# Gated linear attention and an MLP on one core: the last output tile's first half is copied out of PSUM by ScalarE instead of VectorE

## The chip, the cores and the metric

The kernel runs on one core of one Trainium2 chip. The metric is the device time of one execution in microseconds (us), as the median of several runs. A profile of one further execution tells where the time goes; its span runs from the first to the last instruction of the program.

## What is computed

The reference takes `q`, `k`, `v` and `f_logit`, each of 4 batches x 8 heads x 768 steps x 48 channels, and two weight matrices of 384 x 2048 and 2048 x 384, all float32:

```
f = 1 / (1 + exp(-f_logit))
for t in range(768):
    state = f[t, :, None] * state + outer(k[t], v[t])     # 48 x 48 per head
    y[t] = q[t] @ state
x = y with the heads of a step side by side               # 3072 x 384
h = x @ w_in                                              # 3072 x 2048
g = max(h, 0) ** 2
out = g @ w_out                                           # 3072 x 384
```

## The kernel before, in words

**The blocks.** The 768 steps are cut into six blocks of 128 steps; with the four batches a block has 512 columns (`NT`). For each block the attention part leaves x as three tiles of 128 rows (`NJ` = 3), each as a high and a low float16 part. The MLP then runs over 16 groups of 128 hidden channels (`NF` = 16, index `f`).

**The MLP of a block** is `Moe.run` (L354). For each `f`, `up` (L273) makes the hidden tile `ph` in PSUM with nine matmuls on TensorE (L295), `square` (L299) has ScalarE scale, clip, square and round it to `gh`, and `rest` (L335) has VectorE take the rounding remainder `gl`. Some steps later (`lag`), `down` (L344) multiplies `gh` and `gl` with the second weights and adds into three output tiles `po[0]` to `po[2]` in PSUM (L350), one for each 128 output channels (index `e`), nine matmuls for each `f`, three for each `e`. Each `po` is 128 x 512 float32 and fills one PSUM bank.

**The last block** ends in another order (L361 to L371). The `down` matmuls of its last seven `f` are held back and then run output tile by output tile: 21 matmuls for `e` = 0, 21 for `e` = 1, 21 for `e` = 2. Behind the matmuls of each `e` comes a step of the list `ends` (L996), and then the copy of `po[e]`, scaled, from PSUM to the tile `ob_last` in SBUF. `tails(e)` (L436) says in which pieces: one piece for `e` = 0 and `e` = 1, marked 1; for `e` = 2 two halves of 256 columns, the first marked 0 and the second marked 1. Before the change VectorE makes all four copies (L368).

**The flag and the branch.** The fast arithmetic holds for inputs of ordinary size. `verdict` (L1027) gathers on VectorE whether they are, and writes a flag (L1066). The third step of `ends`, which stands between the matmuls of `e` = 2 and the copies of `e` = 2, has every engine load the flag into a register (`values_load`, L999). After `fast_path` comes a branch on that register, `tc.If` (L1184), which every engine takes by itself: where the flag is set, a long general path runs, which has instructions for all engines; in the runs here it is skipped. Behind the branch the pieces of `ob_last` go out to DRAM (L1193), the piece marked 0 on ScalarE's DMA queue and the pieces marked 1 on SP's. Between the last product and the branch TensorE also runs 11 spare matmuls (L1016) whose results nobody reads. The program ends with a round of waits and drains on all engines, which the profile puts at L1250.

**What sets the order.** Each engine works through its own instructions in order. In this part of the kernel the order is that of the source; the written-out orders `FIRST` and `SECOND` concern the beginning only. The Tile framework adds the waits between engines. So on ScalarE the order near the end is: the last `square`, the flag load, the branch, the transfer of L1193; on VectorE: the last `rest`, the verdict, the copies of `e` = 0 and 1, the flag load, the two half copies, the branch.

Of the kernel before, what the change touches and what calls it, by code (L numbers as in the profile page):

```python
# [20 lines left out]
ALU = mybir.AluOpType  # L21
# [28 lines left out]
O_SCALE = 1.0 / (G_SCALE * W_SCALE)  # L50
# [54 lines left out]
class Moe:  # L105
# [248 lines left out]
    def run(self, hooks, obs=None, before=None, lag=LAG, hold=0, ends=()):  # L354


        for n in range(len(self.fs) + lag):
            if before and not obs and n == len(self.fs) + lag - 1:
                return
            self.at = n  # L360
            if obs and n == len(self.fs):  # L361
                for e in range(NJ):
                    for f in self.fs[-lag - hold :]:
                        self.down(f, (e,))
                    if e < len(ends):
                        ends[e]()
                    for _, cs in tails(e):
                        self.nc.vector.tensor_scalar(  # L368
                            out=obs[e][:, cs], in0=self.po[e][:, cs], scalar1=O_SCALE, scalar2=None, op0=ALU.mult
                        )  # L370
                return  # L371
            if n < len(self.fs):
                for hook in hooks.get((n, 0), ()):
                    hook()
                f = self.fs[n]
                self.up(f)
                self.square(f)
                for hook in hooks.get((n, 0.5), ()):
                    hook()
                self.rest(f)  # L380
                for hook in hooks.get((n, 0.7), ()):
                    hook()
            if before and n == 0:
                before()
                self.sums_of()
            if lag <= n < len(self.fs) - hold + (not hold) * lag:
                self.down(self.fs[n - lag])
            for hook in hooks.get((n, 1), ()):
                hook()
# [46 lines left out]
def tails(e):  # L436

    if e < NJ - 1:
        return ((1, slice(0, NT)),)
    return ((0, slice(0, NT // 2)), (1, slice(NT // 2, NT)))  # L440
# [814 lines left out]
```

## Time and profile before

| what | value |
|---|---|
| median of 3 runs | 457.17 us (456.66 to 457.46) |
| the profiled execution, its own time | 457.91 us |
| its span, first to last instruction | 456.2 us |
| TensorE matmuls busy | 447.8 us, 98% of the span |
| TensorE weight loads busy (beside the matmuls) | 225.2 us, 49% |
| ScalarE busy | 292.2 us, 64% |
| VectorE busy | 252.7 us, 55% |
| GpSimd busy | 77.9 us, 17% |
| granted TensorE clock, mean share of full speed | 0.996 |

The time of the profiled execution is longer than its span by 1.7 us, what lies before the first and after the last instruction. PE is TensorE's matmuls and PEld its weight loads, DVE is VectorE, ACT ScalarE, POOL GpSimd, SP the engine that issues most transfers. A name with a q (ACTq, DVEq) stands for that engine's sequencer: loads of registers, branches, semaphore instructions and the issuing of transfers, none of which count as busy. Matmuls follow each other in a pipeline, so their busy time tells little of how fast they run.

### The profile page before, as it was taken

The page shows a single profiled execution, that of the slowest core. Times are in us where ns is not written, and L with a number is a line of the kernel's source. Part 1 is how long each engine was busy: PE and PEld are TensorE (multiplying, and loading weights), DVE is VectorE, ACT ScalarE, POOL GpSimd, SP SyncE. Part 2 cuts the span into 40 slices and gives each one's busy share as a digit, 9 for nine tenths or more (in the row PEclk, how much of TensorE's full clock was granted, in tenths as well). Part 3 has the DMA queues.
Part 4 walks back from the last instruction along what each step waited for, and adds up shares of the span by engine and source line. Part 5 has one row for each costly group of instructions (what it writes and reads, how often), then busy time and mean ns, then how long its engine had stood idle before and what let it go on. Part 6 is the DMA issues. An engine that isn't in the chain of part 4 may idle for free.

```text
span 456.2 us, 11171 instructions
## 1 busy us (share of the span) xinstructions
PE 447.8 (98%) x4558; PEld 225.2 (49%) x4561; DVE 252.7 (55%) x445; ACT 292.2 (64%) x697; POOL 77.9 (17%) x126
## 2 busy tenths in 40 slices
PE   7999899999999999999999999999999999999998
PEld 3655554444454554545554455554455544444443
DVE  7999952879575656836434845535663322323131
ACT  4579856975566674767666877665975553765440
POOL 4446380898000000000000000000000000000000
PEclk9899999999999999999999999999999999999999
DMA  8988319551655424461243443144422000100002
GB/s 271 283 314 281 85 20 332 181 196 24 164 110 147 86 64 120 124 149 30 47 115 97 131 83 102 25 122 112 122 64 42 1 2 17 71 0 1 0 0 79
DMA packets 65821, 48.09 MB, mean 105 GB/s; under 512 B 47968, under 2 KB 51296, under 8 KB 65760
## 3 DMA queue, kind: packets, MB, share of 16 engines
q1 hardware_dynamic: 65168, 46.42, 36.2%
q0 software_dynamic: 448, 0.73, 0.7%
q8 instruction: 38, 0.62, 0.6%
q14 instruction: 23, 0.19, 0.1%
q10 hardware_dynamic: 144, 0.13, 0.1%
HBM read 35.84 MB, written 7.86 MB: 96 GB/s over the span
## 4 chain that ended last, share of the span: by engine, by line
PE 85%; ACT 4%; POOL 4%; DVE 3%; issue 2%; DMA 1%; SPq 0%; POOLq 0%; DVEq 0%
PE po L350 37%; PE ph L295 35%; PE ds L682 2%; POOL w L181 2%; PE ds L663 2%; POOL w L176 1%; PE py L746 1%; DMA vn<-in_vN_dram 1%; PE ph L756 1%; PE ph L746 1%; DVE fkq L552 1%; PE ds L675 1%; PE first_py L728 1%; PE py L756 1%; ACT head L162 1%
## 5 line engine op out<-in xcount | busy, mean ns | idle before, releaser
L295 PE MATMUL ph<-x,w 128*128 128x512 f16 x855 | 198.6, 379 | 0.6 <-DVE gl L337 0.6
L350 PE MATMUL po<-gh,w 128*128 128x512 f16 x570 | 169.7, 379 | 0.3 <-issue 0.3
L337 DVE TENSOR_TENSOR gl<-ph,gh 128x512 f16<-128x512 f32 x94 | 64.8, 690 | 180.0 <-ACT gh L316 180.0
L295 PEld LDWEIGHTS <-w 128*128 128x128 f16 x873 | 84.9, 98 | 102.9 <-issue 1.1
L350 PEld LDWEIGHTS <-w 128*128 128x128 f16 x864 | 82.8, 98 | 98.3
L312 ACT ACTIVATE ph<-ph 128x512 f32<-128x512 f32 x95 | 55.5, 584 | 111.9 <-PE ph L295 111.8
L350 PE MATMUL po<-gl,w 128*128 128x512 f16 x288 | 109.4, 380 | 0.0
L316 ACT ACTIVATE gh<-ph 128x512 f16<-128x512 f32 x94 | 56.1, 597 | 2.9
L313 ACT ACTIVATE ph<-ph 128x512 f32<-128x512 f32 x95 | 55.3, 582 | 3.0
L556 POOL TENSOR_SCALAR fkq<-fkq 128x8 f32<-128x8 f32 x18 | 12.7, 704 | 217.5 <-DVE fkq L552 102.1
L181 POOL TENSOR_TENSOR w<-wa,w 128x384 f16<-128x384 f32 x29 | 30.1, 1040 | 2.0
L176 POOL CAST w<-wa 128x384 f16<-128x384 f32 x29 | 19.8, 685 | 26.6 <-DVE wa L165 22.6
L552 DVE TENSOR_TENSOR_SCAN fkq<-fz,dr 128x520 f32<-128x520 f32 x18 | 23.1, 1282 | 1.9 <-ACT fz L545 1.3
L569 DVE TENSOR_TENSOR_SCAN fkq<-fz,dz 128x520 f32<-128x520 f32 x18 | 22.9, 1274 | 0.6
L165 DVE SCALAR_TENSOR_TENSOR wa<-raw,head 128x384 int32<-128x384 int32 (+1 forms) x33 | 22.9, 727 | 0.2 <-POOL w L181 0.2
L599 ACT COPY sx<-sp 48x208 f32<-48x208 f32 x40 | 14.5, 363 | 12.5 <-DVE sp L712 11.8
L746 PE MATMUL py<-sc,vn 64*48 64x64 f32 (+1 forms) x384 | 21.0, 222 | 0.4 <-DVE sc L697 0.3
L746 PEld LDWEIGHTS py<-sc,vn 64*48 64x48 f32 (+1 forms) x384 | 16.4, 126 | 8.9 <-issue 7.7
L162 ACT ACTIVATE head<-raw 128x384 f16<-128x384 bf16 (+1 forms) x33 | 20.2, 636 | 0.6 <-DMA raw<-in_w_dram 0.5
L756 PE MATMUL py<-rx,sx 48*48 48x64 f32 x192 | 19.9, 216 | 0.2
L316 ACT ACTIVATION_READ_ACCUMULATOR gh<-ph 128x1 f32 x94 | 18.3, 194 | 0.0
L746 PE MATMUL ph<-sc,vn 64*48 64x64 f32 (+1 forms) x256 | 16.6, 222 | 0.0
(146 smaller groups left out, 479.1 us busy)
## 6 DMA issues: line engine op xcount, KB each, us to landing
raw<-in_w_dram SPq DMA_DIRECT2D x33, 383.8 KB, 6.0
fkq<-in_fkqT_dram SPq DMA_DIRECT2D x15, 768.0 KB, 5.3
vn<-in_vN_dram SPq DMA_DIRECT2D x24, 192.0 KB, 4.4
kn<-steps SPq DMA_DIRECT2D x14, 224.0 KB, 3.2
steps<-fkq SPq DMA_DIRECT2D x48, 64.0 KB, 2.2
out_dram<-ob SPq DMA_DIRECT2D x12, 256.0 KB, 2.3
fkq<-in_fkqT_dram SPq DMA_DIRECT2D x9, 256.0 KB, 5.6
last_kq<-fkq SPq DMA_DIRECT2D x28, 64.5 KB, 2.9
```

The costliest lines, as they stand in the source:

```text
L162: nc.scalar.mul(out=self.upper(head, F16), in_=high, mul=TOP_SCALE)
L176: eng.tensor_copy(out=w[:, 0], in_=a)
L181: (eng or nc.vector).tensor_tensor(out=w[:, 1], in0=a, in1=high, op=ALU.subtract)
L295: self.nc.tensor.matmul(self.ph[f], lhsT=w[:, i], rhs=x[:, j], start=first and n == 0, stop=last and n == 2)
L312: nc.scalar.activation(ph, ph, AF.Relu, scale=R_SCALE if self.half else 1.0)
L313: nc.scalar.activation(ph, ph, AF.Square)
L316: nc.scalar.activation(gh, ph, AF.Copy, accum_out=self.sums[:, n : n + 1])
L337: self.nc.vector.tensor_tensor(out=gl, in0=self.ph.pop(f), in1=gh if self.half else gh.bitcast(F32), op=ALU.subtract)
L350: self.nc.tensor.matmul(po[e], lhsT=l, rhs=r, start=f == fs[0] and i == 0, stop=f == fs[-1] and i == 2,)
L552: V.tensor_tensor_scan(out=rr[:, ::-1], data0=self.fz[:, NZ * CZ : 0 : -1], data1=dr[:, ::-1], initial=0.0, op0=ALU.mult, op1=ALU.add,)
L746: nc.tensor.matmul(self.py[c][h * C : h * C + m, b * C : (b + 1) * C], lhsT=self.vn[rows, b, h * D : h * D + m], rhs=self.sc[rows, h, b], ...
L756: nc.tensor.matmul(self.py[c][h * C : h * C + m, b * C : (b + 1) * C], lhsT=s[rows, b * D : b * D + m], rhs=q[rows], start=False, stop=b = ...
```

## The change

In the last block, the piece marked 0 is copied by ScalarE (`nc.scalar.mul`), the pieces marked 1 by VectorE as before. Only `e` = 2 has a piece marked 0, so of the four copies one changes its engine.

```diff
@@ -364,10 +364,14 @@
                         self.down(f, (e,))
                     if e < len(ends):
                         ends[e]()
-                    for _, cs in tails(e):
-                        self.nc.vector.tensor_scalar(
-                            out=obs[e][:, cs], in0=self.po[e][:, cs], scalar1=O_SCALE, scalar2=None, op0=ALU.mult
-                        )
+                    for late, cs in tails(e):
+                        ob, po = obs[e][:, cs], self.po[e][:, cs]
+                        if late:
+                            self.nc.vector.tensor_scalar(
+                                out=ob, in0=po, scalar1=O_SCALE, scalar2=None, op0=ALU.mult
+                            )
+                        else:
+                            self.nc.scalar.mul(out=ob, in_=po, mul=O_SCALE)
                 return
```

## Rows read from the trace of the kernel before

**Rows 1.** The profile page: its first line.

```profile
span 456.2 us, 11171 instructions
```

**Rows 2.** The chain that ended last, 440 to 457 us: start, us, what.

```profile
442.73 9.06 PE po L350 x42
...
451.84 2.35 PE spare L1016 x10
```

**Rows 3.** Timeline, 452.2 to 453 us: start, us, engine line op, [idle before <-releaser].

```profile
451.83 0.76 DVE L368 TENSOR_SCALAR ob_last<-po 128x256 f32<-128x256 f32 x2 [3.84 <-PE po L350]
...
452.28 0.37 ACTq L1193 DMA_DIRECT2D out_dram<-ob_last  x1
452.61 0.33 SPq L1193 DMA_DIRECT2D out_dram<-ob_last  x1
```

**Rows 4.** Groups of instructions by shape, whole span: count | busy us, mean ns.

```profile
L777 ACT CAST x<-py 112x256 f16<-112x256 f32 x12 | 4.6, 385 | 0.0
...
L409 ACT ACTIVATE ob<-po 128x512 f32<-128x512 f32 x8 | 4.3, 593 | 0.0
...
L472 ACT ACT_TABLE_LOAD x1 | 1.3, 1283 | 0.8 <-PEq L1241 0.8
...
L368 DVE TENSOR_SCALAR ob_last<-po 128x256 f32<-128x256 f32 x2 | 0.8, 420 | 3.8 <-PE po L350 3.8
```

**Rows 5.** DMA issues by line: count, KB each, median us from issue to landing.

```profile
out_dram<-ob_last ACTq DMA_DIRECT2D x1, 128.0 KB, 2.1
out_dram<-ob_last SPq DMA_DIRECT2D x1, 128.0 KB, 2.0
```

**Rows 6.** What SP's queue waited for: us in total, times, longest.

```profile
SPq L1250 <- DVEq L1184: 0.3, 1, 0.3
```

**Rows 7.** The branch, L1184, 451.5 to 455: ns min/median/max, first and last start.

```profile
L1184 PEldq COMPARE_BRANCH  x1: 3356/3356/3356, 450.1 to 450.1; - x1
L1184 DVEq COMPARE_BRANCH  x1: 72/72/72, 451.8 to 451.8; - x1
L1184 PEldq EVENT_SEMAPHORE  x1: 51/51/51, 454.2 to 454.2; - x1
L1184 DVEq EVENT_SEMAPHORE  x1: 21/21/21, 454.7 to 454.7; - x1
```

**Rows 8.** Timeline, 440 to 457 us.

```profile
439.84 0.19 ACT L316 ACTIVATION_READ_ACCUMULATOR gh<-ph 128x1 f32 x1
...
440.07 0.69 DVE L337 TENSOR_TENSOR gl<-ph,gh 128x512 f16<-128x512 f32 x1 [1.25 <-ACT gh L316]
...
447.30 0.69 DVE L368 TENSOR_SCALAR ob_last<-po 128x512 f32<-128x512 f32 x1 [3.30 <-PE po L350]
...
447.85 5.09 SPq L1193 DMA_DIRECT2D out_dram<-ob_last  x3
```

**Rows 9.** The flag load, L999: ns min/median/max, first and last start.

```profile
L999 ACTq TENSOR_LOAD <-flag x1: 467/467/467, 443.4 to 443.4; - x1
...
L999 DVEq TENSOR_LOAD <-flag x1: 542/542/542, 447.3 to 447.3; - x1
```

**Rows 10.** The branch, L1184, 443 to 447.65.

```profile
L1184 SPq EVENT_SEMAPHORE  x8: 17/17/17, 447.1 to 447.6; - x8
L1184 ACTq COMPARE_BRANCH  x1: 50/50/50, 444.0 to 444.0; - x1
L1184 POOLq COMPARE_BRANCH  x1: 50/50/50, 444.0 to 444.0; - x1
L1184 SPq COMPARE_BRANCH  x1: 50/50/50, 444.3 to 444.3; - x1
L1184 ACTq EVENT_SEMAPHORE  x1: 17/17/17, 446.4 to 446.4; - x1
```

**Rows 11.** The end of the program, L1250, 444 to 454.65.

```profile
L1250 POOLq DRAIN  x1: 1284/1284/1284, 444.5 to 444.5; - x1
L1250 ACTq DRAIN  x1: 148/148/148, 452.7 to 452.7; - x1
```

## The prediction

> **What bounds the kernel now.** I read the page first, for the span [rows 1], then the chain of waits at the end, then the timeline of each engine there, then the rows of the flag load (L999), of the branch (L1184), of the last transfers (L1193) and of the program's end (L1250). The reader is to see two things.
>
> First, TensorE works without a gap up to the last product: the chain holds 42 L350 matmuls in 9.06 us and leaves them at 451.8 [rows 2]. All the change can touch is what comes after, 456.2 - 451.8 = 4.4 us, and what it puts ahead of a queue that somebody waits for.
>
> Second, that tail is no plain sum of copy and transfer. VectorE's two half copies start at 451.83, each 0.42 us long and overlapping to 0.76 us in all [rows 3, 4]; the first half leaves on ScalarE's queue at 452.28 and the second on SP's at 452.61 [rows 3]. ScalarE's transfer lands 2.1 us after its issue, at 454.4, and SP's 2.0 after, at 454.6 [rows 5]. But SP also waits 0.3 us for VectorE's first semaphore behind the branch [rows 6], which comes at 454.7 although VectorE branched at 451.8 [rows 7]: 2.9 us in which VectorE has nothing recorded. What follows, to 456.2, is the closing round of waits of all engines. So today **VectorE's branch** sets the end, 0.1 to 0.3 us behind the transfers.
>
> **The change, step by step.**
>
> *The first half moves to ScalarE.* Removed: one VectorE copy. VectorE's remaining copy can start at 451.83 instead of behind the first, so it ends some 0.34 us earlier (0.76 less one copy of 0.42), and SP's transfer goes out at about 452.3. By the rows above this is worth nothing: VectorE's branch was already issued at 451.8, together with its first copy and not after its second [rows 3, 7], and that branch ends last. Even given back in full, 0.34 us is under what can be told from no change: 0.2% here is 0.91 us.
>
> *The copy itself.* ScalarE's nearest row is its cast of 112x256 elements out of PSUM, 0.39 us [rows 4]; I take that (0.59, its scaled copy of twice the size at L409, is the upper end). Its function tables were loaded once in the whole program [rows 4], while it has run the scaled copy of L409 eight times for `ob` among its other functions, so no second load is due: 0. ScalarE's last work today ends at 440.03 [rows 8], so no compute is displaced.
>
> *What it is put ahead of.* This is where the cost lies. ScalarE's order today is: load the flag (443.4, 0.47 us) [rows 9], branch (444.0), its first semaphore behind the branch (446.4) [rows 10], then stand at L1193 until VectorE has copied. All this runs beside TensorE's last 8 us and costs nothing. In the source the copy stands behind the flag load and ahead of the branch, so the branch now stands behind an instruction that waits for the last matmul. An engine here passes on to its next instruction only when the one that waits has started: VectorE's flag load is at 447.3, beside its second copy at 447.30, and its branch at 451.8, beside the copy at 451.83 [rows 3, 7 to 9]. So I put ScalarE's branch at 451.85 instead of 444.0.
>
> Behind it stands the time to the first instruction on the other side. The rows have it for ScalarE over the same skipped code: 446.4 - 444.0 = **2.4 us**. The others: SP 2.8 (444.3 to 447.1), POOL 0.5 (444.0 to a drain at 444.5), VectorE 2.9, TensorE 4.1 (450.1 to 454.2, of which part is its wait for the spare matmuls) [rows 7, 10, 11]. I take ScalarE's own. Bounds: 0.5 below, 4.1 above. Then two or three semaphore steps to the transfer: SP shows 447.6 to 447.85, so 0.2 [rows 8, 10].
>
> The sum: 451.85 + 2.4 + 0.2 = 454.45 for ScalarE's transfer, against 452.28; landing 2.1 later, 456.55. SP goes through its waits one by one, 0.07 us each where nothing is outstanding (eight in 447.1 to 447.6 [rows 10]); I count one such step from the landing's wait to where it is free of VectorE's. Today SP is through VectorE's wait at about 454.75, and 456.2 - 454.75 = 1.45 us are left. So the end is 456.55 + 0.07 + 1.45 = 458.1, **1.9 us later**. ScalarE's own closing drain, today at 452.7 [rows 11], comes at about 455 and holds nobody.
>
> The span goes from 456.2 to 458.1 and the profiled execution's own time from 457.91 to 459.8. That execution lies 0.74 us above the median of the three runs, 457.17; put on the median, 1.9 us give **459.1**.
>
> *Do the two copies run side by side?* No row shows two engines reading one PSUM bank together; both halves lie in one bank. Side by side costs nothing; one behind the other, in source order, VectorE would start at 451.83 + 0.39 + 0.04 (the handoff from ScalarE's 440.03 to VectorE's 440.07 [rows 8]) = 452.26. Its branch moves by 0.43 and its first semaphore to 455.1, still ahead of 456.55. So the sum stands either way; the other order would put ScalarE's branch 0.43 us later.
>
> The Trainium skill ("PSUM — Partial Sum Buffer", section "PSUM bank collisions raise a hardware error") speaks against the change here: two engines may not touch one bank of the same partitions together, reads included, and the accesses should be guarded "by bank × quadrant". By that rule VectorE's half has to wait for ScalarE's and the split brings no parallel copying. No row of this trace decides it; the sum is the same by both.
>
> **The rivals.**
>
> *1. The branch is short, and nothing is lost (not slower).* Place: between ScalarE's branch and its transfer. It decides whether ScalarE's landing passes VectorE's 454.7: if branch and semaphores together take under 0.5 us, the transfer is out by 452.6 and the end stays at 456.2. Up to 1.4 us the loss stays under 0.91. For it: POOL went on 0.5 us behind the same branch [rows 10, 11], and ScalarE now stands 8 us ahead of the branch in which something could be got ready. Against: ScalarE itself took 2.4 us, and VectorE took 2.9 after standing 3.84 us ahead of its branch [rows 3, 7]. POOL has next to nothing in the skipped code, ScalarE has loops of activations there. The time: 457.2; with copies one behind the other VectorE's branch ends the kernel 0.43 us later, 457.6.
>
> The Trainium skill ("Runtime: NRT & Kernel Launch", section "Instruction fetch mechanics") has fetching ahead as purely sequential, so that a taken branch to a target outside the window waits for a transfer. By that, standing ahead of the branch helps nothing and only the distance skipped counts, which speaks for 2.4 us and against this rival.
>
> *2. Three branches at once.* ScalarE's and VectorE's branches fall together at 451.8, with TensorE's, begun at 450.1, still open for 3.36 us [rows 7]. If they hold each other up, ScalarE's takes VectorE's 2.9 (+2.4 us, 459.6) or at most TensorE's 4.1 (+3.6 us, 460.8). For it: today SP, which branched 0.3 us after ScalarE, needed 2.8 against 2.4. Against: in that crowd ScalarE's own was the 2.4.
>
> *3. Another order.* Were the flag load also put behind the copy on ScalarE, another 0.47 us would follow: +2.4, 459.6. The load's place in the source and VectorE's order speak against it.
>
> *4. Faster.* By 0.91 us I find no mechanism; only a different order elsewhere in the program, from the moved instruction, could do it.
>
> **How the numbers follow.** The forecast, 459.1, has 0.70, with its own range of 458.6 to 459.6 (the rounding of the rows and the spread of 0.8 us among the runs before). Rivals 2 and 3 have 0.14 together, rival 1 with both prices 0.13, rival 4 0.03. So slower by over 0.2% is 0.84, within 0.2% 0.13, faster 0.03. 0.2%, 0.91 us, is about what a measurement of this kernel tells from no change. The range starts at 458.0, the edge of that, leaving out rivals 1 and 4, and ends at 460.8, the upper bound of the branch.
>
> **What would show it.** Right: ScalarE's copy at L368 at about 451.8, its branch beside it, its first semaphore behind the branch at 454.2 to 454.7, its transfer at about 454.5 instead of 452.28, SP's longest closing wait on that landing and no longer on VectorE, and a tail of 6.3 us behind the last matmul where 4.4 stood. SP's transfer should go out earlier, at 452.3 (or at 452.7 with the copies one behind the other). Wrong: ScalarE's branch still near 444.0, or its transfer before 453; or the span unchanged with VectorE's semaphore last as now. If the branch takes 2.4 and the end still doesn't move, my reading of who ends last is false.

## The result, and the profile after

The changed kernel takes 460.46 us (median of 4 runs, 460.33 to 460.76) against 457.08 us before (also the median of 4 runs, one more than in the table ahead of the prediction), a ratio of 1.0076 (95% interval 1.0064 to 1.0088): 3.4 us slower. The forecast was 459.1, 1.9 us slower. The direction held, and so did the whole range, 458.0 to 460.8; the size is nearly twice the forecast's and lies outside 458.6 to 459.6, the range that the forecast gave to its own sum. Line numbers behind the change are four higher than in the kernel before: L999 is L1003 now, the branch L1184 is L1188, the transfers L1193 are L1197, the closing waits L1250 are L1254.

The first line of the page, which answers to [rows 1]:

```profile
span 458.6 us, 11171 instructions
```

ScalarE's and VectorE's copies and the transfers of the last tile, from timelines of single engines and of the end of the span (start us, us, engine line op, [idle before <-releaser]). They answer to [rows 3]:

```profile
450.55 0.38 ACT L374 ACTIVATE ob_last<-po 128x256 f32<-128x256 f32 x1 [11.79 <-PE po L350]
...
450.56 2.35 PE L1020 MATMUL spare<-one 128*128 128x512 bf16 x10
450.96 0.42 DVE L370 TENSOR_SCALAR ob_last<-po 128x256 f32<-128x256 f32 x1 [4.26 <-ACT ob_last L374]
451.42 0.33 SPq L1197 DMA_DIRECT2D out_dram<-ob_last  x1
453.35 2.32 ACTq L1197 DMA_DIRECT2D out_dram<-ob_last  x1
```

Two things are to be seen. VectorE's half does not run beside ScalarE's: it starts 0.41 us later, and its releaser is ScalarE's copy. And ScalarE's transfer goes out 2.8 us behind the start of the first copy instead of 0.45, and takes **2.32 us to issue** where it took 0.37.

The rows of the branch (ns min/median/max, first and last start), which answer to [rows 7, 10]:

```profile
L1188 PEldq COMPARE_BRANCH  x1: 3416/3416/3416, 448.9 to 448.9; - x1
L1188 ACTq COMPARE_BRANCH  x1: 50/50/50, 450.6 to 450.6; - x1
L1188 DVEq COMPARE_BRANCH  x1: 72/72/72, 451.0 to 451.0; - x1
L1188 PEldq EVENT_SEMAPHORE  x1: 51/51/51, 453.0 to 453.0; - x1
L1188 ACTq EVENT_SEMAPHORE  x1: 17/17/17, 453.1 to 453.1; - x1
L1188 DVEq EVENT_SEMAPHORE  x1: 21/21/21, 453.8 to 453.8; - x1
```

ScalarE's branch now stands beside its copy, and 2.5 us pass to its next instruction. The landings (KB, us from the start of the issue) answer to [rows 5], SP's longest closing wait to [rows 6]:

```profile
out_dram<-ob_last SPq DMA_DIRECT2D x1, 128.0 KB, 2.1
out_dram<-ob_last ACTq DMA_DIRECT2D x1, 128.0 KB, 3.7
```

```profile
SPq L1254 <- DMA out_dram<-ob_last: 4.8, 1, 4.8
```

SP ends on that landing, at 453.35 + 3.7 = 457.05, and no longer on VectorE.

Executions differ by up to 2.2 us in what lies before the last product: over all traces of this document, the first read of the finished last tile starts between 450.42 and 452.66 us (at 451.83 in the profile before and at 450.55 in this one). So below I also compare the **tail**, the span less the start of the first instruction that reads the finished last tile: 456.2 - 451.83 = 4.4 us before and 458.6 - 450.55 = 8.1 us now. The tail is 3.7 us longer, the medians 3.4. One run of all those below, of the kernel with the transfer on another queue, took 938.18 us where its nine others took 456.95 to 458.11, and is left out of every ratio.

### The profile page after: what moved, and what is told of

It reads as the page before. It is cut to its first block, busy times and chain, and to the rows that moved or that the text cites. A ratio compares the mean times of both kernels' runs of the same rounds, so it can differ in the third digit from the quotient of the medians.

```text
span 458.6 us, 11171 instructions
## 1 busy us (share of the span) xinstructions
PE 447.2 (98%) x4558; PEld 224.8 (49%) x4561; DVE 252.1 (55%) x444; ACT 292.7 (64%) x698; POOL 77.9 (17%) x126
## 4 chain that ended last, share of the span: by engine, by line
PE 82%; DVE 6%; POOL 4%; DMA 2%; ACT 2%; issue 2%; SPq 0%; POOLq 0%; DVEq 0%; ACTq 0%
PE po L350 37%; PE ph L295 35%; PE ds L686 2%; POOL w L181 2%; PE ds L667 2%; DMA raw<-in_w_dram 2%; DVE fkq L556 2%; POOL w L176 1%; PE py L750 1%; DVE fkq L573 1%; PE ph L760 1%; PE ph L750 1%; DVE wa L165 1%; PE py L760 1%; ACT head L162 1%
```

## The experiments

Two questions were open. Is it the branch behind the copy that costs (theory 1), or the copies themselves (rival 2)? And why did the transfer take 2 us more to issue? The numbers of theories and rivals in this section are those of the experiments' own expectations; the prediction's rivals are other ones.

**The transfer on another queue.**

```diff
-            (nc.sync if n else nc.scalar).dma_start(out[NBLK - 1, e * P : (e + 1) * P, cs], obs[e][:, cs])
+            nc.sync.dma_start(out[NBLK - 1, e * P : (e + 1) * P, cs], obs[e][:, cs])
```

> The changed kernel, but the first half of the last tile leaves on SP's queue, which has branched long before. ScalarE still copies it and still branches late. Theory 1 (what costs is that ScalarE's transfer stands behind ScalarE's branch): nothing waits for ScalarE's branch any more, both transfers are out by 1 us behind the last product, and the end is set by VectorE's branch, which starts 0.4 us later than before because its copy waits for ScalarE's: 457.3 to 457.7. Rival 2 (what costs is the copy on ScalarE and VectorE's wait for it): the time stays near 460.4.

Measured: 457.82 us (457.78 without the run of 938.18) against 456.83 for the kernel before in the same session, ratio 1.0022 (1.0012 to 1.0032). Its last two transfers, its branches and what SP waited for:

```profile
451.12 0.90 SPq L1197 DMA_DIRECT2D out_dram<-ob_last  x2
```

```profile
L1188 ACTq COMPARE_BRANCH  x1: 50/50/50, 450.7 to 450.7; - x1
L1188 DVEq COMPARE_BRANCH  x1: 72/72/72, 451.1 to 451.1; - x1
...
L1188 DVEq EVENT_SEMAPHORE  x1: 21/21/21, 454.3 to 454.3; - x1
```

```profile
SPq L1254 <- DVEq L1188: 1.7, 1, 1.7
```

ScalarE copies and branches as late as in the changed kernel, and 2.4 of the 3.4 us are gone: theory 1 holds, rival 2 falls. What is left, 1.0 us, is a little more than expected (457.3 to 457.7). VectorE's branch sets the end here: it starts 0.4 us behind the first copy, and takes 3.2 us to its semaphore, 0.3 more than before.

**The wait alone.** The kernel before, with one added ScalarE instruction behind the flag load:

```diff
-            lambda: general.append(nc.values_load(general[0][0:1, 0:1], min_val=0, max_val=1)),
+            lambda: (general.append(nc.values_load(general[0][0:1, 0:1], min_val=0, max_val=1)), nc.scalar.mul(out=moe.const.tile([P, 1], F32, name="column"), in_=moe.po[2][:, :1], mul=O_SCALE)),
```

> The kernel before, VectorE making all copies, with one added ScalarE instruction ahead of the branch: it scales one column (128x1) of the last output tile out of PSUM into a place that nobody reads. So ScalarE waits for the last product, and no copy changes its engine. Theory 1: ScalarE's branch comes 7.9 us later as in the changed kernel, and the first half leaves as late as there: 460.1 to 460.7. Rival 2: VectorE's copies come about 0.25 us later behind the small one, nothing else: 457.3.

Measured: 460.67 us, ratio 1.0081 (1.0064 to 1.0098), no different from the changed kernel. The profiled execution is the longest of its four (462.54); what it has more lies before the last product, and its tail is 460.8 - 452.66 = 8.1 us as in the changed kernel. In its trace ScalarE's read of one column and its transfer, VectorE's copies, and ScalarE's branch and first semaphore:

```profile
452.66 0.17 ACT L999 ACTIVATE column<-po 128x1 f32<-128x1 f32 x1 [11.79 <-PE po L350]
455.49 2.39 ACTq L1193 DMA_DIRECT2D out_dram<-ob_last  x1
```

```profile
452.86 0.76 DVE L368 TENSOR_SCALAR ob_last<-po 128x256 f32<-128x256 f32 x2 [4.04 <-ACT column L999]
```

```profile
L1184 ACTq COMPARE_BRANCH  x1: 50/50/50, 452.7 to 452.7; - x1
...
L1184 ACTq EVENT_SEMAPHORE  x1: 17/17/17, 455.3 to 455.3; - x1
```

No copy has changed its engine here. An instruction of 0.17 us that waits for the last product ahead of ScalarE's branch is enough for the whole loss. VectorE's copies wait for it too, 0.2 us, although it writes a tile of its own: what the two share is `po`, which both only read.

**The copy behind the branch.** The reverse: ScalarE copies, but branches early.

```diff
-                            self.nc.scalar.mul(out=ob, in_=po, mul=O_SCALE)
+                            self.owing = ob, po
...
+        ob, po = moe.owing
+        nc.scalar.mul(out=po, in_=ob, mul=1 / O_SCALE)
+    ob, po = moe.owing
+    nc.scalar.mul(out=ob, in_=po, mul=O_SCALE)
```

The first two added lines at the end stand inside the skipped general path, the last two behind the branch; the PSUM pool of this tile is opened outside the fast path so that it lives on (lines left out here).

> The changed kernel with ScalarE's copy moved behind the branch (the PSUM tile is kept until then; the general path, which is skipped, puts its own result back into it). ScalarE branches early again, at about 443 to 444. Its copy now stands behind VectorE's in the source, so it would run 0.45 us behind the last product, and its transfer goes out at 0.9 us behind it. Theory 1 with theory 3 (first transfer slow where its engine has not stood at it): issue of 2.3 us and a landing 3.7 us after it, 458.3 to 458.9. Theory 1 with rival 4 (slow only right behind a branch): issue of 0.4 us, 456.9 to 457.4. Rival 2: near 460.

Measured: 456.99 us against 456.83, ratio 1.0001 (0.9991 to 1.0012). The timelines of VectorE and ScalarE:

```profile
450.81 0.42 DVE L370 TENSOR_SCALAR ob_last<-po 128x256 f32<-128x256 f32 x1 [3.84 <-PE po L350]
```

```profile
451.31 0.39 ACT L1196 ACTIVATE ob_last<-po 128x256 f32<-128x256 f32 x1 [12.30 <-DVE ob_last L370]
451.73 0.37 ACTq L1201 DMA_DIRECT2D out_dram<-ob_last  x1
```

The whole loss is gone with ScalarE still copying, and here too the copies run one behind the other, VectorE's first. The transfer, the only one that ScalarE issues in the program, takes 0.37 us although ScalarE had not stood at it: so a transfer is not slow for being the first on its queue.

**An earlier transfer on ScalarE's queue.** The changed kernel with:

```diff
-            lambda: None,
+            lambda: nc.scalar.dma_start(aside.tile([P, C], F32, name="unread"), mask),
```

> The changed kernel, with one small transfer (128 x 64 float32 from SBUF to a scratch place in DRAM that nobody reads) issued on ScalarE's queue ahead of the flag load, while ScalarE is idle. The slow issue at the end was 2.32 us where it had been 0.37. Theory 3 (the first transfer of the program on a queue is slow to issue, unless its engine has stood at it before): the last one is now the second, 0.4 us, lands 2.1 us after its issue, and the time falls by 1.6 to 2.0 us to 458.4 to 458.9. Rival 4 (it is slow because it comes right behind a branch): 460.4 as before.

Measured: 460.02 us, ratio 1.0078 (1.0061 to 1.0095). ScalarE's two transfers in its timeline:

```profile
437.95 0.34 ACTq L1002 DMA_DIRECT2D unread<-mask  x1
...
453.26 2.13 ACTq L1197 DMA_DIRECT2D out_dram<-ob_last  x1
```

The first transfer of the queue takes 0.34 us and the second, behind the branch, 2.13. Theory 3, that a queue's first transfer is slow, falls; what is left is rival 4, the branch just ahead.

**The branch by itself, without the crowd.** The kernel before; ScalarE reads a column of the middle tile ahead of its branch, and the first tile goes out on its queue.

```diff
-            lambda: general.append(nc.values_load(general[0][0:1, 0:1], min_val=0, max_val=1)),
+            lambda: (general.append(nc.values_load(general[0][0:1, 0:1], min_val=0, max_val=1)), nc.scalar.mul(out=moe.const.tile([P, 1], F32, name="column"), in_=moe.po[1][:, :1], mul=O_SCALE)),
...
-            (nc.sync if n else nc.scalar).dma_start(out[NBLK - 1, e * P : (e + 1) * P, cs], obs[e][:, cs])
+            (nc.sync if n and e else nc.scalar).dma_start(out[NBLK - 1, e * P : (e + 1) * P, cs], obs[e][:, cs])
```

> The kernel before, with an added ScalarE read of one column of the middle output tile ahead of ScalarE's branch, so that this branch comes about 4 us before the end of the products, with no other engine's branch open, and with the transfer of the first output tile put on ScalarE's queue, its data ready long before. What is read is how long that transfer, ScalarE's first behind the branch, takes to issue. Theory 5 (a transfer soon behind a branch is slow by itself): 2.0 to 2.5 us. Rival 6 (it is slow because ScalarE's, VectorE's and TensorE's branches fall together): 0.3 to 0.6 us. The time itself stays near 457 by both, since the transfer of the last tile's first half waits for its data anyway.

Measured: 458.82 us in one run (456.94 before). The rows of the branch and of ScalarE's two transfers (ns min/median/max, first and last start):

```profile
L1184 ACTq COMPARE_BRANCH  x1: 50/50/50, 447.1 to 447.1; - x1
L1184 PEldq COMPARE_BRANCH  x1: 3376/3376/3376, 449.2 to 449.2; - x1
L1184 ACTq EVENT_SEMAPHORE  x1: 17/17/17, 449.9 to 449.9; - x1
```

```profile
L1193 ACTq DMA_DIRECT2D out_dram<-ob_last x2: 405/1268/2132, 450.1 to 452.4; - x2
```

ScalarE branches 2.1 us before TensorE and 3.8 us before VectorE, and the first transfer behind its branch still takes 2.13 us, the next 0.41. TensorE's and VectorE's branches are open by the time of this transfer, but so they are in the run with the copy behind the branch (449.1 and 450.8), where it took 0.37. Rival 6, the crowd, falls. The time missed what both had given it, near 457: the last tile's first half, issued in 0.41 us, landed only 3.7 us later. Why is open.

**Both halves on ScalarE's queue.** The changed kernel with `(nc.sync if e < NJ - 1 else nc.scalar)` at L1197.

> The changed kernel with both halves of the last tile leaving on ScalarE's queue, one behind the other. Theory 5, in the form that the first transfer behind the branch pays once: first issue 2.0 to 2.4 us, second 0.3 to 0.5 us, time 460.5 to 461.2. If each transfer near the branch pays: two slow issues, 462.0 to 463.0. Rival 6 gives the same as the first form, since the branches still fall together.

Measured: 460.23 us in one run, a little under the expected band.

```profile
L1197 ACTq DMA_DIRECT2D out_dram<-ob_last x2: 384/1204/2023, 453.6 to 455.7; - x2
```

The first transfer behind the branch pays 2.02 us, the second 0.38.

**Small work between branch and transfer.** The changed kernel with eight, then 32 one-column copies:

```diff
+    for n in range(8):
+        nc.scalar.mul(out=sums[:, n : n + 1], in_=obs[0][:, n : n + 1], mul=1.0)
```

> The changed kernel with eight one-column ScalarE copies (of the first output tile, into a place that nobody reads afterwards) between ScalarE's branch and its transfer, some 1 to 1.5 us of work. Theory 5a (something for the transfer arrives a fixed time behind the branch): the copies run at once at some 0.17 us each, the transfer's issue is shorter by what they took, 0.8 to 1.3 us, and the time stays at 460.0 to 460.7. Theory 5b (the first transfer behind the branch costs 2 us whenever it comes): the issue stays at 2.1 to 2.4 us and the time is 1 to 1.5 us longer, 461.2 to 462. If the copies themselves stall for some 2 us, it is not the transfer but any instruction there.

> The run with eight small ScalarE copies behind the branch, with 32 of them, 0.09 us apart, some 2.9 us in all. There the issue of ScalarE's transfer began earlier or later in the runs but ended 4.8 to 5.2 us behind ScalarE's branch each time. Theory 5a (a transfer of ScalarE can't go out before about 5 us behind its branch, other work can): the copies run without a stall, the transfer begins at 5 to 5.7 us behind the branch and its issue takes 0.3 to 0.6 us. Rival 7 (the stretch of code itself arrives in two pieces, and what stands some way behind the target waits, whatever it is): one of the copies stands still for 1 to 2 us.

Measured: 460.5 us with eight (456.94 before) and 461.38 us with 32 (456.87 before), one run each. ScalarE's timeline of the one and of the other:

```profile
453.71 0.48 ACT L1195 ACTIVATE sums<-ob_last 128x1 f32<-128x1 f32 x4 [2.35 <-ACTq L1188]
454.07 1.83 ACTq L1199 DMA_DIRECT2D out_dram<-ob_last  x1
454.10 0.47 ACT L1195 ACTIVATE sums<-ob_last 128x1 f32<-128x1 f32 x4
```

```profile
451.80 0.38 ACT L374 ACTIVATE ob_last<-po 128x256 f32<-128x256 f32 x1 [11.79 <-PE po L350]
454.49 2.24 ACT L1195 ACTIVATE sums<-ob_last 128x1 f32<-128x1 f32 x23 [2.31 <-ACTq L1188]
456.55 0.37 ACTq L1199 DMA_DIRECT2D out_dram<-ob_last  x1
456.64 0.93 ACT L1195 ACTIVATE sums<-ob_last 128x1 f32<-128x1 f32 x9
```

The copies never stall. With eight of them the transfer begins 3.1 us behind the branch, not 2.8, and its issue is 1.83 us, 0.5 shorter; with 32 it begins 4.75 us behind ScalarE's branch (at 451.80, beside its copy) and takes 0.37. Theory 5a holds, that ScalarE's transfer does not get out before about 5 us behind the branch while other work runs; rival 7, that the code behind the branch arrives in two pieces and whatever stands in the second has to wait, falls. In the seven kernels where a ScalarE transfer comes soon behind ScalarE's branch, the issue ends at 5.1, 5.0, 5.2, 5.2, 4.8, 4.9 and 5.1 us behind the branch (the changed kernel, the early transfer, the wait alone, the branch by itself, both halves, eight copies, 32 copies).

**SP made to wait instead of ScalarE.** The kernel before, with a small SP transfer ahead of the branch, of 64 columns of the last tile's first half:

```diff
-                moe.run(hooks[k], obs, owed, LAST_LAG, HOLD, ends)
+                moe.run(hooks[k], obs, owed, LAST_LAG, HOLD, ends); nc.sync.dma_start(aside.tile([P, C], F32, name="unread"), obs[NJ - 1][:, :C])
```

> The kernel before, with one small transfer on SP's queue ahead of the branch that reads the first half of the last tile out of SBUF into a scratch place in DRAM that nobody reads. So SP, and not ScalarE, stands ahead of its branch until the last product is copied; three large transfers wait behind SP's branch, two of them with their data ready. By theory 1 it is the same loss on another engine: SP's branch 0.4 to 0.5 us behind the last product, 2.8 us to its first semaphore, 0.75 us of semaphores, then the transfers. Theory 5a for every engine: the first of them takes 1 to 2 us to issue, and the time is 462.5 to 464. Rival 8 (ScalarE alone is slow there; in the runs so far SP's first transfer came 3.2 us behind its branch and took 0.34): 0.3 to 0.4 us each, and 461 to 462.3.

Measured: 462.3 us in one run (456.87 before), the upper end of what rival 8 gave.

```profile
L1184 SPq COMPARE_BRANCH  x1: 50/50/50, 451.9 to 451.9; - x1
```

```profile
L1184 SPq EVENT_SEMAPHORE  x8: 17/17/17, 454.6 to 455.1; - x8
```

```profile
L1193 SPq DMA_DIRECT2D out_dram<-ob_last x3: 338/420/473, 455.3 to 456.2; - x3
```

```profile
L1193 ACTq EVENT_SEMAPHORE  x2: 17/28/38, 455.0 to 455.1; - x2
L1193 ACTq DMA_DIRECT2D out_dram<-ob_last x1: 392/392/392, 455.2 to 455.2; - x1
```

The loss of theory 1 comes on this engine too: the branch 0.8 us behind the last product, the first transfer 3.4 us behind the branch. But SP issues it at the usual pace, in 0.34 us. Rival 8 holds: the 2 us at the transfer are ScalarE's. The late branch of SP seems to hold ScalarE's transfer as well, though the profile names no releaser: ScalarE branched at 443.2 and its data were copied by 451.5, yet its semaphore instructions ahead of the transfer come at 455.0 and 455.1, beside SP's behind SP's branch.

**VectorE's copies behind the branch.** The kernel before, with both half copies moved:

```diff
-                    for _, cs in tails(e):
+                    for _, cs in tails(e) if e < NJ - 1 else ():
...
+        nc.vector.tensor_scalar(out=last, in0=obs[NJ - 1], scalar1=1 / O_SCALE, scalar2=None, op0=ALU.mult)
+    for _, cs in tails(NJ - 1):
+        nc.vector.tensor_scalar(out=obs[NJ - 1][:, cs], in0=last[:, cs], scalar1=O_SCALE, scalar2=None, op0=ALU.mult)
```

As above, the first added line stands in the general path, and the pool of the tile is opened further out; `last` is the PSUM tile `po[2]`.

> The kernel before, with VectorE's two half copies of the last tile moved behind the branch (the PSUM tile is kept until then; the general path, which is skipped, puts its own result back into it). VectorE then branches about 4 us earlier, beside its second copy, and no transfer moves: issues 0.45 and 0.8 us behind the last product. If VectorE's branch sets the end of the kernel before, as the prediction has it, the end moves up to the landing of SP's last transfer, 0.1 to 0.2 us, which is 456.6 to 456.8 against 456.8 before and no verdict; the trace then shows SP's last wait on a landing and none on VectorE. If it does not set the end: the same tail of 4.4 us behind the last product.

Measured: 456.44 us against 456.94, ratio 0.9991 (0.9979 to 1.0003). The branch, the copies and SP's wait:

```profile
L1185 DVEq COMPARE_BRANCH  x1: 72/72/72, 447.7 to 447.7; - x1
```

```profile
451.56 0.76 DVE L1192 TENSOR_SCALAR ob_last<-po 128x256 f32<-128x256 f32 x2 [3.84 <-PE po L350]
```

```profile
SPq L1254 <- PEq L1185: 0.7, 1, 0.7
```

The tail is 455.5 - 451.56 = 3.94 us where it was 4.37, and SP waits for TensorE's branch at the end instead of VectorE's. So VectorE's branch did set the end of the kernel before, in its trace. The time itself tells no difference; among all versions run, none is faster by more than can be told.

## Why the prediction was right, and where its size was off

*VectorE's branch sets the end today, and an earlier second copy is worth nothing.* The first is right: with that branch early, the tail is 0.4 us shorter. The second no run shows, since the second copy never came earlier: SP's transfer goes out 0.87 us behind the first copy's start, 0.78 before.

*ScalarE's branch moves behind the wait for the last product.* Right, and shown three times: by the wait alone (460.67), by the copy behind the branch (456.99) and by the transfer on SP's queue (457.82).

*From the branch to the next instruction, 2.4 us.* It was 453.1 - 450.6 = 2.5, after ScalarE had stood 8 us ahead of the branch, so rival 1, a short branch, is out. (Its bound of 0.5 us is the branch alone: 451.85 + 0.5 + 0.2 = 452.55.) The trace also has DMA packets of the kind `instruction`, and one of 8 KB starts at 451.47, 0.9 us behind ScalarE's branch. The Trainium skill ("Runtime: NRT & Kernel Launch", section "Instruction fetch mechanics") has a taken branch to a target outside the window of fetched code wait for a DMA that fetches it, and gives no time for this. The trace agrees, and gives the 2.5 us.

*The copies, side by side or not.* They run one behind the other, VectorE's start 0.41 us behind ScalarE's (0.43 in the prediction). The Trainium skill ("PSUM — Partial Sum Buffer", section "PSUM bank collisions raise a hardware error") asks for a guard between two such accesses, and the trace agrees that there is one: VectorE's releaser is ScalarE's copy. What the bank would do without that wait no run shows. As forecast, it changes nothing here, since VectorE's semaphore comes at 453.8 and the landing at 457.05; on SP's queue it is part of the remaining 1.0 us.

*The landing, 2.1 us after the issue.* **This term failed.** It was taken from a transfer whose engine had branched 8 us before. Behind a fresh branch ScalarE's issue takes 2.32 us instead of 0.37, and the landing comes 3.7 us after its start. With that, the prediction's own sum meets the span: 453.35 + 3.7 + 0.07 + 1.45 = 458.6. The tail was forecast at 6.3 us and is 8.1; 1.6 of the 1.8 us between them are this term, and the rest of the sum is right within 0.2. That the whole range held is luck: it was drawn up to 460.8 for a branch of 4.1 us, the prediction's rival 2, and that did not occur: three branches fell together and ScalarE's took 2.5. No rival of the prediction had a slower issue in it.

What stays open is why ScalarE's transfer does not get out before about 5 us behind its branch. Ruled out are the first use of the queue, the other engines' branches, a stall of whatever instruction stands there, and a cost that comes however late the transfer is (all but the first by one run each). SP, at 3.4 us behind a late branch, has no such delay. I did not find what differs between the two.

One candidate stands in the traces and was not tested. In the changed kernel five 8 KB packets of the kind `instruction` start behind the first copy, and three where ScalarE branches early (the kernel before, the copy behind the branch). By their order in time the two more are ScalarE's: one at 451.47, the other at 453.73, 0.6 us behind ScalarE's first semaphore. In the six kernels with a slow issue, that issue ends 1.2 to 1.5 us behind the end of the second one, as the first semaphore comes 1.1 to 1.3 us behind the end of the first. So the transfer may wait for the second piece of code, though the small copies did not. Against it stands SP: behind its late branch the second packet runs from 455.14 to 455.50, and its first transfer is issued by 455.64.

## What to carry to other kernels

Before moving work to an idle engine, look at what that engine issues afterwards: an instruction that waits for the last result holds everything behind it in that engine's order, and here a taken branch and the transfer behind it took 5 us on ScalarE and 3.7 on SP, once nothing covered them. A duration read from a row holds for the state in which the engine was; a transfer behind a branch long past says nothing of one right behind it. Putting the late work behind the branch gave the whole loss back here, and putting the transfer on a queue whose engine had already branched gave 2.4 of the 3.4 us.

## What was not expected

ScalarE's first transfer behind a taken branch takes 1.8 to 2.4 us to issue in the six kernels where it begins within 3.1 us of the branch, ending 4.8 to 5.2 us behind the branch, while small copies on the same engine run there at once, 0.09 us apart, and SP's transfers take 0.34 to 0.47 us. VectorE's way over the branch is not constant either. In the kernel with its copies behind the branch, its first semaphore there:

```profile
L1185 DVEq EVENT_SEMAPHORE  x1: 21/21/21, 451.1 to 451.1; - x1
```

That is 3.4 us behind its branch at 447.7, where it was 2.9 us before, 2.8 in the changed kernel and 3.2 with the transfer on SP's queue. The `instruction` packet that follows the branch starts at 449.32 here, 1.6 us behind it, and at 452.88 in the kernel before, 1.0 us behind it.
